# Attention and MLP on one core: loads in 512-byte runs, and a new order of the first steps

## The chip, the cores and the metric

The kernel runs on one core of a Trainium2 chip. The metric is the time of one execution in microseconds (us), measured on the device; for each kernel the median of several runs is given. Five engines of the core work side by side, each through its own queue and in the order in which its instructions stand there: TensorE (PE, with its weight loads as PEld) does the matrix products, VectorE (DVE) and ScalarE (ACT) the work on elements, GpSimd (POOL) element work that doesn't touch PSUM, and SyncE (SP) issues transfers. Matrix products land in PSUM, everything else lies in SBUF.

## The reference

Kernelized attention with random features, then a gated MLP on its output:

```python
q_s, k_s = (q * scale, k * scale)
def phi(x):
    proj = np.einsum('bhsd,md->bhsm', x, omega)
    sq = np.sum(x * x, axis=-1, keepdims=True) / 2.0
    h = proj - sq
    h = h - np.max(h, axis=-1, keepdims=True)
    return np.exp(h) / np.sqrt(m)
q_p, k_p = (phi(q_s), phi(k_s))
kv = np.einsum('bhsm,bhsd->bhmd', k_p, v)
z = np.sum(k_p, axis=2)
num = np.einsum('bhsm,bhmd->bhsd', q_p, kv)
den = np.einsum('bhsm,bhm->bhs', q_p, z)[..., None] + 1e-06
...
g = x @ w_gate
silu = g * (1.0 / (1.0 + np.exp(-g)))
out = silu * (x @ w_val) @ w_out
```

q, k and v have 8 batches, 8 heads, 576 positions and 64 dimensions in float32; omega has 128 features. The MLP sees 4608 rows of 512 and is 1536 wide. Its weights arrive as 64-bit floats, and the kernel makes float32 of them from their halves.

## The kernel before

**Groups and steps.** A group is two heads (a pair) by 256 positions, or, for the last 64 positions of each head, one group of all eight heads ("rest"). Each batch has 9 groups of keys and 9 of queries. A step handles two groups. The first AHEAD = 6 steps take two key groups each; from step 6 on a step pairs one query group with one key group; the last ones have two query groups. There are 72 steps.

**One step of the attention.** load (L340) brings the step's q and k rows into nat, load_v (L348) its v rows into one of eight tiles that have a column of ones behind each head's 64 columns (L311 to L314). load_group (L325) puts positions 2p and 2p + 1 of the group on partition p, one transfer of 128 KB for a full group, four for a rest group. st_transpose (L363) transposes nat on PE (pt), squares it on POOL (sq, L377) and copies the transposed rows on ACT (x, L378). st_project (L382) multiplies by omega on PE (pp, L393; its 16 records are one step's). st_max (L399) sums the squares on DVE (L404), takes the rows' maxima from PSUM (L411), and makes the bias of the exponentials of both with two small instructions (L413, L414). st_exp (L417) makes eight exponentials on ACT (ph, L425). k_accumulate (L510) adds the products of ph and v on PE to kvacc, two steps later; the ones give z as column 64. When a batch's four heads are complete, kv_finalize (L438) copies kvacc to SBUF (kvr); for batches 4 to 7 it also has PE transpose z (zp, L447) and sends it through memory to all partitions (zt, L464). q_transpose, q_mult, q_den, q_norm and q_out make the attention's output of ph of the queries.

**Buffers that tie the steps together.** nat has three buffers, so the load for step n + 3 waits for step n's transposes and squares. The projection of an even early step uses the two buffers of ps_p, that of an odd one two of ps_m's four; each is free again when the step's exponentials are done.

**Weights.** convert_all (L247) is a generator. Each of the 36 pieces loads 512 KB raw (load_raw, L218), takes the absolute value on ACT (L260), five DVE instructions (L262 to L270), a POOL addition (L272), and for the first nine pieces a split in a high and a low part (L242, L243); a copy goes to memory (L275). A tick advances it by one of seven stages. How many ticks are due when step n ends is interpolated over `clock` between `marks` (L202), pairs of a step and a number of pieces: (0, 0), (21, 6), (23, 9) and more. Step 21 (EARLY) is the first at which the MLP has its input.

**What sets the order of the work.** The program issues a step's parts in the order CLOSE before step 21 and GROUPED after it, with ticks and MLP work between them (L798 to L814). From that program a list scheduler makes each engine's final order at build time by its own estimate of when an instruction is ready; the chip runs each queue in that order. So an instruction whose data come later than estimated holds up those behind it on its engine. Ahead of the loop (L790 to L797) stand the loads of steps 0 to 2, omega's setup (L301: two transfers into both halves of a tile, a transpose, a scaled copy omT) and v of step 0, all issued by SP. The MLP (stream, L683) multiplies with high and low parts, three products for one (mm1 L641, mm2 L650).

Of the kernel before, what the change touches and what calls it, by code (L numbers as in the profile page):

```python
# [11 lines left out]
F32 = mybir.dt.float32  # L12
# [11 lines left out]
def kernel(  # L24
# [16 lines left out]
    P = 128  # L41
# [83 lines left out]

    def pairs_of(gr):
        return [(2 * c, 2 * c + 1) for c in range(CH)] if gr is None else [gr[:1]] * CH

# [89 lines left out]
    def load_raw(n):  # L218
        if n < 3 * NF:
            f, i = divmod(n, 3) if n >= 3 * FA else (n % FA, n // FA)  # L220
            w = (wg32, wv32, wo32)[i]
            raw = att.tile([P, 2 * DM], I32, name=f"st{f}_{i}", tag="stw")
            raws[n] = f, i, raw
            if i < 2:
                nc.sync.dma_start(
                    raw.rearrange("p (c f) -> p c f", f=2 * P),
                    w[:, f * 2 * P : (f + 1) * 2 * P].rearrange("(c p) f -> p c f", p=P),
                )
            else:
                nc.sync.dma_start(raw, w[f * P : (f + 1) * P, :])  # L230

    weights = {}
    converted = set()
# [66 lines left out]

    def setup_omega():  # L301
        om2 = accp.tile([P, 2, D], F32, name="om2", tag="acc")
        for j in range(2):
            nc.sync.dma_start(om2[:, j, :], omega)
        pt = ps_moe("pt_om", [P, M])
        nc.tensor.transpose(pt, om2.rearrange("p a d -> p (a d)"), ident)
        nc.scalar.activation(omT, pt, AF.Copy, scale=SCALE)

    vtile = [att.tile([P, CH, 2, VW], F32, name=f"v{i}", bufs=1) for i in range(NVF)]  # L311
    vrest = [att.tile([P, 2 * CH, 2, VW], F32, name=f"vrest{i}", bufs=1) for i in range(1)]
    for t in vtile:
        nc.gpsimd.memset(t[:, :, :, D:VW], 1.0)  # L314
    for t in vrest:
        nc.gpsimd.memset(t, 0.0)
        for c in range(CH):
# [4 lines left out]
    nats = {}  # L322
    busy = []

    def load_group(t, src, b, gr, v_):  # L325
        if gr is not None:
            pr, r = gr
            nc.sync.dma_start(
                t[:, :, :, 0:D],
                src[b, 2 * pr : 2 * pr + 2, r : r + G, :].rearrange("h (p c) d -> p c h d", c=CH),  # L330
            )
            return
        for c in range(CH):
            for j, pr in enumerate(pairs_of(gr)[c]):
                nc.sync.dma_start(
                    t[j * RES : (j + 1) * RES, 2 * c + j if v_ else c, :, 0:D],
                    src[b, 2 * pr : 2 * pr + 2, S - RES : S, :].rearrange("h p d -> p h d"),
                )
# [6 lines left out]
            for i, b, _, gr in slots(n, kind):  # L345
                load_group(nats[n][:, i], src, b, gr, False)

    def load_v(n):  # L348
        for i, b, g, gr in slots(n, "k"):
            rest = gr is None  # L350
            ts = (vtile, vrest)[rest]
            t = ts[nv[rest] % len(ts)]
            nv[rest] += 1
            assert t not in busy, "v's tile is still needed"
            busy.append(t)
            vrows[b, g] = t
            load_group(t, v, b, gr, True)

    box = {}
    sts = {}  # L360
# [38 lines left out]
    def st_max(n):  # L399
        if n >= NS:  # L400
            return
        st, sq, pp = sts[n]

        nc.vector.tensor_reduce(  # L404
            st[:, 0].rearrange("p i c h -> p (i c h)"),
            sq.rearrange("p i c h d -> p (i c h) d"),
            axis=AX.X,
            op=ALU.add,
        )
        for hh in range(2):  # L410
            nc.vector.tensor_reduce(st[:, 1, :, :, hh], pp[hh], axis=AX.X, op=ALU.max, negate=True)  # L411
        s0, s1, s2, s3 = (st[:, j].rearrange("p i c h -> p (i c h)") for j in range(4))
        nc.vector.scalar_tensor_tensor(s2, s0, SQC, s1, op0=ALU.mult, op1=ALU.add)  # L413
        nc.vector.scalar_tensor_tensor(s3, s0, -SQC, s2, op0=ALU.mult, op1=ALU.add)  # L414
        return True
# [21 lines left out]

    def kv_finalize(b, a2):  # L438
        acc = kvacc.pop((b, a2))
        raw = att.tile([P, 4, VW], F32, name=f"kvr{b}_{a2}", tag="kvr", bufs=4)  # L440
        nc.scalar.copy(raw, acc)
        for j in range(2):
            kvst[b, 2 * a2 + j] = raw[:, 2 * j : 2 * j + 2, :]
        if b >= BPOOL:

            zp = ps_att(f"zp{b}_{a2}", [4, P])
            nc.tensor.transpose(zp, raw[:, :, D], ident)  # L447
# [23 lines left out]
    def q_den(n):  # L471

        n -= JLAG
        for _, b, g, gr in slots(n, "q"):
# [10 lines left out]
            else:  # L485
                pr = gr[0]
                zt = zbc[b, pr // 2][:, 2 * (pr % 2) : 2 * (pr % 2) + 2, :]
                nc.gpsimd.tensor_tensor(
                    jk, ph, zt.rearrange("p (o h) m -> p o h m", o=1).broadcast_to([P, CH, 2, M]), op=ALU.mult
                )  # L490
            dn = att.tile([P, 3, CH, 2], F32, name=f"dj{b}_{g}", tag="dj", bufs=6)
            nc.vector.tensor_reduce(dn[:, 0], jk, axis=AX.X, op=ALU.add)
# [17 lines left out]
    def k_accumulate(n, half):  # L510
# [3 lines left out]
        for b, g, gr, c in ks[half * len(ks) // 2 : (half + 1) * len(ks) // 2]:  # L514
# [4 lines left out]
            for j, pr in enumerate(pairs_of(gr)[c]):  # L519
                a2 = pr // 2  # L520
                first = (b, a2) not in kvacc
                if first:
                    kvacc[b, a2] = ps_k.tile([P, 4, VW], F32, name=f"kvacc{b}_{a2}", tag="kv")
                acc = kvacc[b, a2]
                done.setdefault((b, a2), []).append(pr)
                last = LAST[pr] == (g, c)
                for hh in range(2):
                    nc.tensor.matmul(  # L528
                        acc[:, 2 * (pr % 2) + hh, :],
                        ph[:, c, hh * M : (hh + 1) * M],  # L530
                        vt[:, 2 * c + j if gr is None else c, hh, :],
                        start=first and hh == 0,
                        stop=last,
                        skip_group_check=True,
                    )
                if len(done[b, a2]) == NACC:
                    kv_finalize(b, a2)
# [4 lines left out]

    def q_transpose(n):
        m = n
        todo = [(b, g) for _, b, g, gr in slots(n - TLAG, "q") if b < BPOOL]
        todo += [(b, g) for _, b, g, gr in slots(n - NLAG, "q") if b >= BPOOL]
        for b, g in todo:
            ph = box.pop(("q", b, g))
            pt = (ps_moe if m < EARLY else ps_att)(f"ptq{b}_{g}", [P, 2, G])
            for hh in range(2):  # L550
                for c in range(CH):
                    nc.tensor.transpose(pt[:, hh, c * P : (c + 1) * P], ph[:, c, hh * M : (hh + 1) * M], ident)  # L552
# [294 lines left out]
```

## Time and profile before

| what | us |
|---|---|
| median of 3 runs | 1251.25 |
| lowest and highest run | 1250.28 and 1261.83 |
| the profiled execution, its time | 1254.07 |
| the profiled execution, first to last instruction (span) | 1252.3 |
| PE busy in it | 1217.5 |
| DVE, ACT, POOL busy | 530.8, 599.4, 506.3 |
| mean granted clock of PE | 0.988 |

A line of the timeline gives the start in us, the length in us, the engine, the line of the kernel, the operation, the tile written and the tiles read with their shape, and how many instructions were merged; in brackets stands how long the engine was idle before and for what it waited. SPq is SP's queue issuing a transfer. In the table of stretches each engine has its busy time with the number of instructions, then come the granted clock of PE (1.00 is full), the mean busy share of the 16 DMA engines, and GB/s. In the groups by line "| busy us, mean ns | idle us" stand behind the count; in the list of waits the total, the times and the longest.

### The profile page before, as it was taken

Reading aid. Unit: us, or ns where it says so; the run is one execution under the profiler, and the core shown is the slowest. Engines: PE = TensorE matmul, PEld = TensorE weight load, DVE = VectorE, ACT = ScalarE, POOL = GpSimd, SP = SyncE. Lnnn points to the kernel's source line nnn. Section 1 sums busy time; section 2 is a strip of 40 time slices with the busy share of each in tenths; the row PEclk is TensorE's granted clock in tenths of the full one; section 3 lists DMA queues with packets and bytes.
Section 4 is the critical chain, followed back from the end, with each engine's and each line's share of the span. In section 5 each row is a group of like instructions: output and inputs, shape, how many; then the busy total and the mean of one; then the engine's idle time right before and its main releaser. Section 6 shows DMA issues by size and latency. Waiting matters only on the chain.

```text
span 1252.3 us, 19047 instructions
## 1 busy us (share of the span) xinstructions
PE 1217.5 (97%) x7137; PEld 1013.1 (81%) x7137; DVE 530.8 (42%) x1080; ACT 599.4 (48%) x1344; POOL 506.3 (40%) x448
## 2 busy tenths in 40 slices
PE   6999999999999999999999998999999999999998
PEld 5988877888778888778788876888787778888887
DVE  4887696556752344334434342233433311111112
ACT  3787755554354554556555443564644323221211
POOL 3333443645362213445544432554654314242421
PEclk7999999999999999999999998999999999999999
DMA  6555555343442222222222321221211111010112
GB/s 162 146 122 157 149 135 176 105 141 115 127 126 64 53 71 64 66 66 63 73 52 60 82 52 31 69 59 52 58 43 34 36 24 51 26 51 26 51 31 54
DMA packets 157692, 97.80 MB, mean 78 GB/s; under 512 B 119680, under 2 KB 132000, under 8 KB 157600
## 3 DMA queue, kind: packets, MB, share of 16 engines
q1 hardware_dynamic: 157600, 96.59, 29.0%
q8 instruction: 56, 0.92, 0.3%
q14 instruction: 36, 0.29, 0.1%
HBM read 77.66 MB, written 18.89 MB: 77 GB/s over the span
## 4 chain that ended last, share of the span: by engine, by line
PE 68%; DVE 2%; POOL 1%; ACT 1%; issue 0%; DMA 0%; SPq 0%; POOLq 0%; DVEq 0%
PE o L650 19%; PE g L641 19%; PE v L641 19%; PE pp L393 3%; PE kvacc L528 2%; PE ptq L552 2%; PE xt L607 2%; PE pt L370 1%; PE po L569 1%; POOL hl L725 1%; DVE st L266 0%; DMA nat<-in_k_dram 0%; DVE sl L721 0%; ACT ph L425 0%; DVE st L411 0%
## 5 line engine op out<-in xcount | busy, mean ns | idle before, releaser
L725 POOL TENSOR_TENSOR hl<-sl,hh 128x512 fp32r<-128x512 f32 (+1 forms) x120 | 142.3, 1190 | 208.0 <-ACT hh L724 207.9
L641 PE MATMUL g<-xh,whi 128*128 128x512 f32 (+1 forms) x480 | 181.6, 379 | 1.7 <-DVE sl L721 1.7
L641 PE MATMUL v<-xh,whi 128*128 128x512 f32 (+1 forms) x480 | 180.1, 375 | 2.7 <-DVE acc L674 2.7
L641 PE MATMUL g<-xh,wlo 128*128 128x512 f32 (+1 forms) x480 | 178.1, 372 | 0.0
L641 PE MATMUL g<-xl,whi 128*128 128x512 f32 (+1 forms) x480 | 178.1, 371 | 0.0
L243 POOL TENSOR_TENSOR wlo<-wraw,whi 128x512 fp32r<-128x512 f32 x108 | 139.0, 1299 | 95.6 <-ACT whi L242 94.1
L641 PE MATMUL v<-xh,wlo 128*128 128x512 f32 (+1 forms) x480 | 177.4, 370 | 0.0
L641 PE MATMUL v<-xl,whi 128*128 128x512 f32 (+1 forms) x480 | 177.3, 369 | 0.0
L650 PE MATMUL o<-whi,hh 128*128 128x512 f32 x432 | 173.4, 401 | 2.8 <-ACT hh L724 2.8
L425 ACT ACTIVATE ph<-pp,st 128x128 f32<-128x128 f32 x576 | 157.9, 384 | 32.8 <-DVE st L414 32.5
L650 PE MATMUL o<-whi,hl 128*128 128x512 f32 x432 | 170.6, 395 | 2.4 <-POOL hl L725 2.4
L650 PE MATMUL o<-wlo,hh 128*128 128x512 f32 x432 | 169.8, 393 | 0.0
L724 ACT CAST hh<-sl 128x512 fp32r<-128x512 f32 (+1 forms) x120 | 69.5, 581 | 207.5 <-DVE sl L721 207.1
L721 DVE TENSOR_TENSOR sl<-v,sl 128x512 f32<-128x512 f32 (+1 forms) x120 | 75.7, 633 | 181.3 <-PE v L641 179.3
L674 DVE TENSOR_TENSOR acc<-o,acc 128x512 f32<-128x512 f32 x108 | 74.1, 689 | 185.1 <-PE o L650 185.0
L377 POOL TENSOR_TENSOR sq<-nat 128x512 f32<-128x512 f32 x72 | 77.8, 1081 | 179.2 <-DMA nat<-in_k_dram 132.0
L411 DVE TENSOR_REDUCE st<-pp 128x4 f32<-128x512 f32 x144 | 93.7, 683 | 51.2 <-PE pp L393 51.0
L242 ACT CAST whi<-wraw 128x512 fp32r<-128x512 f32 x108 | 66.4, 623 | 100.0 <-PE v L641 61.2
L641 PEld LDWEIGHTS v<-xh,whi 128*128 128x128 f32 x480 | 90.6, 189 | 20.1 <-DVE acc L674 3.1
L641 PEld LDWEIGHTS g<-xh,whi 128*128 128x128 f32 x480 | 90.9, 190 | 19.7 <-issue 2.7
L641 PEld LDWEIGHTS g<-xh,wlo 128*128 128x128 f32 x480 | 91.0, 190 | 16.0 <-issue 0.4
L641 PEld LDWEIGHTS v<-xh,wlo 128*128 128x128 f32 x480 | 90.5, 189 | 15.2
(67 smaller groups left out, 1886.0 us busy)
## 6 DMA issues: line engine op xcount, KB each, us to landing
wraw<-wscr SPq DMA_DIRECT2D x108, 256.0 KB, 2.7
wscr<-wc SPq DMA_DIRECT2D x36, 256.0 KB, 2.3
out_dram<-acc SPq DMA_DIRECT2D x72, 128.0 KB, 2.3
nat<-in_k_dram SPq DMA_DIRECT2D x64, 128.0 KB, 3.0
v<-in_v_dram SPq DMA_DIRECT2D x64, 128.0 KB, 3.0
nat<-in_q_dram SPq DMA_DIRECT2D x64, 128.0 KB, 2.7
st<-in_moe_w_gate_dram SPq DMA_DIRECT2D x12, 512.0 KB, 5.2
st<-in_moe_w_val_dram SPq DMA_DIRECT2D x12, 512.0 KB, 4.2
```

Source lines behind the costliest of these rows:

```text
L242: nc.scalar.copy(hi, raw)
L243: nc.gpsimd.tensor_tensor(lo, raw, hi.bitcast(F32), op=ALU.subtract)
L377: nc.gpsimd.tensor_tensor(sq, nat, nat, op=ALU.mult)
L393: nc.tensor.matmul(pp[hh][:, i, c, :], x[r, i, c * P : (c + 1) * P], omT[r], start=True, stop=True)
L411: nc.vector.tensor_reduce(st[:, 1, :, :, hh], pp[hh], axis=AX.X, op=ALU.max, negate=True)
L425: nc.scalar.activation(ph[:, c, hh * M : (hh + 1) * M], pp[hh][:, i, c, :], AF.Exp, bias=st[:, 3, i, c, hh : hh + 1], scale=1.0,)
L641: nc.tensor.matmul(ps, a_[:, ws], b_[:, c, :], start=n == 0, stop=n == 3 * NC - 1)
L650: nc.tensor.matmul(ps, a_[:, ts_], b_, start=first and n == 0, stop=last and n == 2)
L674: nc.vector.tensor_tensor(a_, po, a_, op=ALU.add)
L721: nc.vector.tensor_tensor(h, pv, h, op=ALU.mult)
L724: nc.scalar.copy(hh, h)
L725: nc.gpsimd.tensor_tensor(hl, h, hh.bitcast(F32), op=ALU.subtract)
```

## The change

Six edits. (1) load_group takes both positions of a partition as one run: nat and v are laid out by head and then position, so a run is 128 elements or 512 bytes and not 64 or 256. Head and position change places in everything computed from them; `place` says which index is which. (2) For this v's tile holds per head a one, the 64 columns of the even position, the 64 of the odd one, and a one; a product takes the 65 columns that end or begin with a one. kvacc gets 66 columns, z is the sum of columns 0 and 65, and POOL adds them after the copy in kv_finalize. (3) st_max issues the maxima ahead of the squares' sums, and in the first six steps the scheduler may not turn that round. (4) omega's load is one transfer issued by ACT, and the first v's loads are issued by ACT. (5) The marks get a pair (4, 0): no ticks are due ahead of step 4. (6) The first raw weight load is pinned behind the SP instruction that stands ahead of it in the program.

```diff
+    def place(gr, c, hh):
+        return (c, hh) if gr is None else (hh, c)
...
-    marks = [(0, 0.0), (EARLY, 2 * FA), (EARLY + 2, 3 * FA)]
+    marks = [(0, 0.0), (AHEAD - 2, 0.0), (EARLY, 2 * FA), (EARLY + 2, 3 * FA)]
...
+            if n == 0:
+                tc.keep_in_program_order(got)
...
-        for j in range(2):
-            nc.sync.dma_start(om2[:, j, :], omega)
+        nc.scalar.dma_start(om2, omega.rearrange("m (o d) -> m o d", o=1).broadcast_to([M, 2, D]))
...
-    vtile = [att.tile([P, CH, 2, VW], F32, name=f"v{i}", bufs=1) for i in range(NVF)]
+    vtile = [att.tile([P, 2, 1 + CH * D + 1], F32, name=f"v{i}", bufs=1) for i in range(NVF)]
...
-            nc.sync.dma_start(
-                t[:, :, :, 0:D],
-                src[b, 2 * pr : 2 * pr + 2, r : r + G, :].rearrange("h (p c) d -> p c h d", c=CH),
+            eng.dma_start(
+                t[:, :, 1 : 1 + CH * D] if v_ else t.rearrange("p h c d -> p h (c d)"),
+                src[b, 2 * pr : 2 * pr + 2, r : r + G, :].rearrange("h (p c) d -> p h (c d)", c=CH),
             )
...
-        nc.vector.tensor_reduce(
+        for hh in range(2):
+            top = nc.vector.tensor_reduce(st[:, 1, :, :, hh], pp[hh], axis=AX.X, op=ALU.max, negate=True)
+        sums = nc.vector.tensor_reduce(
...
-        for hh in range(2):
-            nc.vector.tensor_reduce(st[:, 1, :, :, hh], pp[hh], axis=AX.X, op=ALU.max, negate=True)
+        if n < AHEAD:
+            tc.add_manual_dep(
+                sums.ins,
+                top.ins.name,
...
-        raw = att.tile([P, 4, VW], F32, name=f"kvr{b}_{a2}", tag="kvr", bufs=4)
-        nc.scalar.copy(raw, acc)
+        both = att.tile([P, 4, 1 + VW], F32, name=f"kvr{b}_{a2}", tag="kvr", bufs=4)
+        nc.scalar.copy(both, acc)
+        raw = both[:, :, 1:]
+        nc.gpsimd.tensor_tensor(raw[:, :, D], raw[:, :, D], both[:, :, 0], op=ALU.add)
...
+                    e, o = place(gr, c, hh)
+                    z = 0 if gr is not None and c == 0 else 1
                     nc.tensor.matmul(
-                        acc[:, 2 * (pr % 2) + hh, :],
-                        ph[:, c, hh * M : (hh + 1) * M],
-                        vt[:, 2 * c + j if gr is None else c, hh, :],
+                        acc[:, 2 * (pr % 2) + hh, z : z + VW],
+                        ph[:, e, o * M : (o + 1) * M],
+                        vt[:, 2 * c + j, hh, :] if gr is None else vt[:, hh, c * VW : (c + 1) * VW],
...
-    for n in range(2):
-        load(n)
-        if n == 0:
-            setup_omega()
+    load(0)
+    setup_omega()
+    load(1)
     for n in range(LAV):
-        load_v(n)
+        load_v(n, nc.scalar)
```

The other lines of the diff put `place` into q_transpose, turn the order of the broadcast in q_den, and give the tiles of v two memsets where one was.

More of the change, by code (lines that the diff above doesn't have):

```diff
@@ L409, in st_max @@
         )
-        for hh in range(2):
-            nc.vector.tensor_reduce(st[:, 1, :, :, hh], pp[hh], axis=AX.X, op=ALU.max, negate=True)
+        if n < AHEAD:
+            tc.add_manual_dep(
+                sums.ins,
+                top.ins.name,
+                mybir.DependencyInfo(mybir.DependencyClass.NoSync, mybir.DependencyReason.DATA),
+                reason="the first maxima are waited for, these sums are not",
+            )
         s0, s1, s2, s3 = (st[:, j].rearrange("p i c h -> p (i c h)") for j in range(4))
@@ L551, in q_transpose @@
                 for c in range(CH):
-                    nc.tensor.transpose(pt[:, hh, c * P : (c + 1) * P], ph[:, c, hh * M : (hh + 1) * M], ident)
+                    e, o = place(gr, c, hh)
+                    nc.tensor.transpose(pt[:, hh, c * P : (c + 1) * P], ph[:, e, o * M : (o + 1) * M], ident)
             qts[b, g] = att.tile([P, 2, G], F32, name=f"qt{b}_{g}", tag="qt")
```

23 lines of the change are left out of this document (12 added, 11 removed).

## The prediction

> **What bounds the kernel now.** First the page's head and the busy time by stretch, to see where TensorE (PE) isn't the bound.
>
> ```profile
> span 1252.3 us, 19047 instructions
> ...
> PE 1217.5 (97%) x7137; PEld 1013.1 (81%) x7137; DVE 530.8 (42%) x1080; ACT 599.4 (48%) x1344; POOL 506.3 (40%) x448
> ...
> 16.00:18.00 2.00, 0.00 (x0) 0.00 (x0) 1.21 (x4) 0.00 (x0) 0.00 (x0) 0.52 1.11 341
> ...
> 30.00:32.00 2.00, 2.00 (x15) 1.78 (x13) 1.14 (x2) 0.03 (x1) 0.00 (x0) 0.50 0.01 5
> ...
> 34.00:36.00 2.00, 2.00 (x25) 1.88 (x25) 1.44 (x3) 1.97 (x8) 1.29 (x1) 1.00 0.27 59
> 46.00:111.00 65.00, 62.02 (x580) 56.06 (x579) 54.17 (x138) 52.91 (x163) 24.96 (x22) 0.97 0.57 144
> 111.00:1252.00 1141.00, 1121.19 (x6309) 926.32 (x6308) 451.80 (x896) 524.37 (x1116) 463.79 (x393) 1.00 0.27 72
> ```
>
> After 111 us PE is busy 1121 of 1141 us, from 46 to 111 us 62 of 65. The matrix work there is unchanged, so it moves as a block: what the start gives or takes is what the end shows. At 16 to 18 us only DVE works, and the granted clock of PE (the column after POOL) falls to 0.52; it is still 0.50 at 30 to 32 us and 1.00 from 34 on. So second the timeline of PE at the start, by steps of the attention (pp x16 is one step's projection; the first row is steps 0 and 1, then 2, 3, 4, 6 and 8).
>
> ```profile
> 7.99 3.79 PE L393 MATMUL pp<-omT,x 64*128 64x128 f32 x32
> ...
> 13.30 0.96 PE L370 MATMUL pt<-ident,nat 128*128 128x128 f32 x4 [0.48 <-DMA nat<-in_k_dram]
> 19.29 2.48 PE L528 MATMUL kvacc<-v,ph 128*128 128x65 f32 x10 [5.03 <-ACT ph L425]
> 21.70 2.67 PE L393 MATMUL pp<-omT,x 64*128 64x128 f32 x16
> ...
> 28.75 2.08 PE L393 MATMUL pp<-omT,x 64*128 64x128 f32 x16
> ...
> 33.93 1.16 PE L393 MATMUL pp<-omT,x 64*128 64x128 f32 x16
> ...
> 41.48 1.16 PE L393 MATMUL pp<-omT,x 64*128 64x128 f32 x16
> ...
> 48.95 1.16 PE L393 MATMUL pp<-omT,x 64*128 64x128 f32 x16
> ```
>
> PE stands 5.03 us for the first exponentials (ph), then projects at half pace (2.67 and 2.08 us against 1.16) until step 4. Steps 0 and 1 (3.79 for two) ran at half pace too, though the profile shows 1.00 there. Third, why ph is late: ScalarE (ACT) and VectorE (DVE) in order of time.
>
> ```profile
> 12.91 0.58 ACT L378 COPY x<-pt 128x512 f32<-128x512 f32 x1 [4.23 <-PE pt L370]
> 18.32 0.66 ACT L260 ACTIVATE wc<-st 128x512 f32<-128x512 f32 x1 [4.83 <-DMA st<-in_moe_w_gate_dram]
> 18.88 4.22 ACT L425 ACTIVATE ph<-pp,st 128x128 f32<-128x128 f32 x16
> ...
> 12.59 0.69 DVE L404 TENSOR_REDUCE st<-sq 128x8 f32<-128x512 f32 x1 [3.37 <-POOL sq L377]
> 13.19 1.28 DVE L411 TENSOR_REDUCE st<-pp 128x4 f32<-128x512 f32 x2
> 15.01 0.69 DVE L404 TENSOR_REDUCE st<-sq 128x8 f32<-128x512 f32 x1 [0.54 <-POOL sq L377]
> ...
> 16.29 0.15 DVE L414 SCALAR_TENSOR_TENSOR st<-st 128x8 f32<-128x8 f32 x1
> ```
>
> Two queues are in the wrong order. On DVE the maxima of step 0 (13.19) stand behind the squares' sums of step 2 (12.59), which wait for step 2's keys; the projection they read ended about 1.9 us after 7.99. On ACT the exponentials have their bias at 16.44 and stand behind the first weight conversion (L260), which waits 4.83 us for a weight load. Fourth, what loads first.
>
> ```profile
> 0.74 1.28 ACT L307 ACT_TABLE_LOAD   x1 [0.74 <-PEq L831]
> ...
> 0.88 0.33 POOL L314 MEMSET v<- 128x4 f32 x8
> ...
> 4.88 1.04 POOL L377 TENSOR_TENSOR sq<-nat 128x512 f32<-128x512 f32 x1 [2.40 <-DMA nat<-in_k_dram]
> ...
> 0.75 1.45 SPq L328 DMA_DIRECT2D nat<-in_k_dram  x2
> 2.24 1.11 SPq L304 DMA_DIRECT2D om<-in_omega_dram  x2
> 3.39 1.30 SPq L328 DMA_DIRECT2D nat<-in_k_dram  x2
> 4.74 1.34 SPq L328 DMA_DIRECT2D v<-in_v_dram  x2
> ...
> 26.69 0.38 SPq L225 DMA_DIRECT2D st<-in_moe_w_gate_dram  x1
> ...
> L464 SPq DMA_DIRECT2D zt<-zd x8: 325/332/348, 404.0 to 901.3; - x8
> ```
>
> An issue of 256 B runs keeps SP 0.65 us, one of 1 KB runs 0.38, one of 512 B runs (zt) 0.33.
>
> **The change, part by part.**
>
> *Omega and first v on ScalarE.* SP loses 1.11 + 1.34 us of issues: step 1's keys go out 1.15 us earlier, step 2's and all behind them 2.45. ACT takes three issues of about 0.65 ahead of its table load; 0.74 + 2.0 + 1.28 = 4.0 us, before omega's transpose gives it work, so they are hidden. If that cover went, each would cost its 0.65. Omega no longer holds PE until 5.18: the transposes of step 0 start with its keys, 4.8. They and step 1's (0.25 each at half pace) and the copy of x end near 6.9, so pp starts at 6.9 instead of 7.99.
>
> The pages have a rule against this edit: the Trainium skill, "DMA: Bandwidth & Descriptors", section "Issuing engines are not separate DMA queues", says that transfers from several engines interleave on the same 16 DMA engines and only issue time is saved. By it omega and v would delay step 0's keys; at the 341 GB/s of the row at 16 us their 320 KB last 1 us, and the time below would be 1 us longer. Here SP alone issues, so no row shows it.
>
> *Maxima before sums.* pp of step 0 ends at 6.9 + 1.9 = 8.8; maxima 1.28, sums 0.69, two small ones 0.31: bias at 11.1. The copy of x for step 2, which ACT has ahead of the exponentials (12.91 before), then waits for PE (pp of step 1 to 10.7, transposes about 1): 11.3 to 12.0. I take the exponentials' start between the two, 11.6 instead of 18.88: **-7.3 us**, from -6.9 to -7.8. The first projection that needs the buffers they free (step 2) followed 2.8 us behind and still does: 14.4 instead of 21.70. What is late next is that release, then the clock.
>
> *The clock.* Step 2 to 6 took 41.48 - 21.70 = 19.8 us, mostly at half clock; step 4 to 8 took 48.95 - 33.93 = 15.0 at full clock. The drop at 16 us came in the gap of PE from 14.26 to 19.29. Now PE has transposes of steps 2 and 3 until about 12.5 and the first ph at 12, so the gap nearly closes: **-4.8 us**, or 0 if the clock falls anyway.
>
> *Weights from step 4.* Two costs. The first load comes when the exponentials of steps 4 and 5 are queued behind L260; who waits for those is the projection two steps on and PE behind it. The wait is between 0 and the 4.83 us of today; in the row at 18.32 it hit with its full length because the order of ACT counts on a load's estimated landing; this load has the shorter queue ahead, so I take 1.0: **+1.0**. Then conversion: up to step 6 the due ticks are 14 before (2 a step), now 8 (2.47 a step from step 4, rounded up); step 21 wants 42 either way. So 6 ticks of 7 a piece move into steps 7 to 20.
>
> ```profile
> L270 DVE SCALAR_TENSOR_TENSOR wc<-st,wc 128x512 f32<-128x512 uint32 x21 | 17.7, 844 | 0.2
> L266 DVE SCALAR_TENSOR_TENSOR st<-st,wc 128x512 int32<-128x512 int32 x21 | 15.4, 732 | 0.2
> L262 DVE TENSOR_SCALAR wc<-wc 128x512 f32<-128x512 f32 x22 | 12.8, 580 | 15.1 <-ACT wc L260 15.0
> L268 DVE TENSOR_SCALAR wc<-st 128x512 int32<-128x512 int32 x21 | 11.0, 523 | 0.2
> L264 DVE TENSOR_SCALAR wc<-wc 128x512 int32<-128x512 int32 x21 | 10.0, 478 | 0.1
> ```
>
> A piece is 844 + 732 + 580 + 523 + 478 = 3157 ns of DVE, six sevenths are 2.7 us. DVE is busy 54.2 of 65 us there and PE 62, so between 0 and 2.7; I take **+1.2**, nearer to hidden.
>
> *Runs of 512 B.* SP saves about 0.3 us on each of 192 big loads (0.65 to 0.33 or 0.38). On the path are only the first: step 0's second load goes out 0.3 earlier, at most -0.5 in all. The rest is hidden behind PE:
>
> ```profile
> PE pt L370 <- DMA nat<-in_k_dram: 1.0, 2, 0.5
> ...
> PE o L650 <- ACT hh L724: 2.8, 1, 2.8
> ...
>   PEld zp L447: 1.0, 4
> ...
> 745.37 3.11 POOL L484 TENSOR_TENSOR jk<-ph,zt 64x256 f32<-64x256 f32 x4 [5.64 <-ACT ph L425]
> ```
>
> PE waits 1.0 us in all for keys, so I take 0; if that cover were gone the gain would grow by the same 1.0. The new place of heads and chunks in ph changes no shape. Eight more memsets (0.33 us for eight) lie in POOL's idle 2.40 ahead of 4.88.
>
> *The second column of ones.* Sixteen small POOL additions behind the copy of kvacc. For batches under 4 the sum is needed steps later. For the other eight finalizations PE transposes z right behind the copy (PEld waits 1.0 us in 4 of them), so the addition now stands between. Its price is not in the trace: from 0 (PE has MLP work to put first) to 8 times a POOL in the middle of the 3.11 us group, 26 us. Near the small end, **+0.5**.
>
> **The sum.** -7.3 - 4.8 + 1.0 + 1.2 + 0.5 = -9.4 us. The profiled execution lasted 1254.07 (span 1252.3 and 1.8 around it), which becomes 1244.7. It lies 2.8 above the median of the runs, 1251.25, so for the median I predict 1241.9, 0.75% faster.
>
> **The rivals.**
>
> *Half clock stays.* If PE's pauses before the exponentials still add up, the 4.8 are lost: 1251.25 - 7.3 + 2.7 = 1246.7. For it: PE was busy from 19.29 on and the clock was still 0.50 at 32 us. Against: the pause falls from 5.03 to under 1 us. The Trainium skill, "TensorE: Matmul & The Clock Gate", section "What's actually happening", says that an idle window of about 3.4 us halves the clock; the trace agrees (5.03 us of pause, 0.52 in the row of 16 us).
>
> *All costs hidden, and later waits shorter too.* L260 finds its weights landed, the ticks hide, and the one long late wait of PE (2.8 us for hh) goes because loads land sooner: 1251.25 - 7.8 - 4.8 - 0.5 - 2.8 = 1235.4. For it: DVE has 11 us free from 46 to 111. Against: that wait hangs on an order of issue.
>
> *No gain.* Loads not pinned (the second weight load) are moved ahead of keys, or the new order only moves the waiting to step 2's data: 1251. Against: the waits removed are of known length.
>
> *Slower: z behind POOL.* The instruction order lets PE reach z's transpose while POOL still has a queue ahead of the addition. At 3.11 + 0.2 us for each of eight finalizations: 1241.9 - 0.5 + 26.5 = 1267.9. It decides from 2.8 us each on ((12.5 + 9.9) / 8 for +1%). For it: nothing else on POOL is ordered for this. Against: a wait of one such place would have to repeat at all eight.
>
> **How the numbers follow.** Chances: the forecast 0.50 (its own range 1237 to 1246), half clock 0.20, all hidden 0.17, no gain 0.08, slower 0.05. A measurement of this kernel tells about 1%, 12.5 us, from no change. Faster by over 1% means under 1238.7: all hidden (0.17) and the lower part of the forecast (0.18), 0.35. Slower by over 1%: 0.05. The rest 0.60. The range holds the forecast, half clock and most of all hidden: 1231 to 1249; left out are no gain, slower, and tails.
>
> **What would show it.** Right: exponentials starting at 11 to 12.5 us with no weight conversion ahead; no pause of PE over 2 us before 20 us; granted clock 1.00 from 14 us on; pp of step 6 near 29 to 31 us; SP issues of q, k and v at 0.33 to 0.4. Wrong: a wait of ACT for the gate weights of several us near 20 to 26 us; pp still over 2 us at step 3; DVE over 9 tenths in steps 7 to 20 with the lead shrinking; PEld waiting over 5 us in all at zp.

## The result, and the profile after

| kernel | median, us | lowest and highest | runs |
|---|---|---|---|
| before | 1251.1 | 1248.4 and 1261.8 | 18 |
| after | 1269.8 | 1261.9 and 1281.5 | 18 |

The ratio is 1.0136, with a 95% interval of 1.0117 to 1.0155: the change makes the kernel slower, by 18.7 us in the medians and by 17 in the ratio, where 9.3 us faster was predicted. Where an execution of a series was disturbed, its ratio leaves it out, and so do the medians of e8, e10 and e11 below. The profiled execution of the kernel after lasted 1262.65 us, near the fast end. Its span is 8.6 us longer than that of before, and these 8.6 are what the trace can place; no trace shows where a median run loses the rest.

First the head of the page after, then the busy time by stretch (columns as in the prediction; the one after POOL is PE's granted clock).

```profile
span 1260.9 us, 19088 instructions
...
PE 1227.1 (97%) x7137; PEld 1016.5 (81%) x7137; DVE 542.3 (43%) x1080; ACT 600.1 (48%) x1344; POOL 514.3 (41%) x472
```

```profile
12.00:14.00 2.00, 0.00 (x0) 0.00 (x0) 1.58 (x5) 0.00 (x0) 0.00 (x0) 0.70 0.88 242
16.00:18.00 2.00, 1.27 (x8) 0.83 (x6) 0.00 (x0) 1.69 (x6) 0.68 (x1) 0.50 0.36 99
30.00:32.00 2.00, 2.00 (x11) 1.92 (x10) 0.00 (x0) 0.00 (x0) 0.00 (x0) 0.50 0.44 127
38.00:40.00 2.00, 2.00 (x18) 1.82 (x15) 0.87 (x2) 0.24 (x1) 0.00 (x0) 0.50 0.80 210
46.00:111.00 65.00, 60.34 (x562) 54.01 (x561) 60.53 (x138) 52.68 (x161) 33.39 (x31) 0.97 0.57 164
111.00:1252.00 1141.00, 1127.40 (x6358) 929.85 (x6355) 463.65 (x909) 530.26 (x1137) 469.22 (x405) 1.00 0.25 71
```

Behind 111 us PE is busy nearly all the time, as before. The loss lies ahead: 7.8 of the 8.6 us are there when step 20 is projected (113.8 against 106.0 us, in the table further down). The clock falls by 14 us already and is still 0.50 at 38 to 40 us; before it was at 1.00 from 34 on. Then PE's timeline, the rows that answer to those of the prediction.

```profile
6.84 3.25 PE L403 MATMUL pp<-omT,x 64*128 64x128 f32 x32
...
14.88 1.34 PE L380 MATMUL pt<-ident,nat 128*128 128x128 f32 x4 [4.20 <-DMA nat<-in_k_dram]
16.95 0.80 PE L403 MATMUL pp<-omT,x 64*128 64x128 f32 x4 [0.73 <-ACT x L388]
...
33.05 0.80 PE L403 MATMUL pp<-omT,x 64*128 64x128 f32 x4 [0.73 <-ACT x L388]
...
45.36 0.49 PE L403 MATMUL pp<-omT,x 64*128 64x128 f32 x4 [0.73 <-ACT x L388]
```

The first projection starts at 6.84, as forecast (6.9). Then PE stands 4.20 us again, now for the keys of step 3. Step 2 is projected at 16.95 instead of 21.70, but step 6 at 45.36 instead of 41.48. The reason is in ACT's order, here its timeline.

```profile
10.78 0.59 ACT L388 COPY x<-pt 128x512 f32<-128x512 f32 x1 [3.25 <-PE pt L380]
16.31 0.58 ACT L388 COPY x<-pt 128x512 f32<-128x512 f32 x1 [4.95 <-PE pt L380]
16.79 4.24 ACT L442 ACTIVATE ph<-pp,st 128x128 f32<-128x128 f32 x16
28.25 0.58 ACT L388 COPY x<-pt 128x512 f32<-128x512 f32 x1 [7.22 <-PE pt L380]
32.41 0.58 ACT L388 COPY x<-pt 128x512 f32<-128x512 f32 x1 [3.58 <-PE pt L380]
32.89 4.24 ACT L442 ACTIVATE ph<-pp,st 128x128 f32<-128x128 f32 x16
...
37.57 0.66 ACT L269 ACTIVATE wc<-st 128x512 f32<-128x512 f32 x1 [0.17 <-DMA st<-in_moe_w_gate_dram]
```

The bias of step 0 is ready at 12.65 (the small DVE instruction of L431, 0.15 us from 12.50); no weight conversion stands ahead of the exponentials. But the copies of x for steps 2 and 3 do, and the second waits 4.95 us for step 3's transposes. The same pattern repeats: x of steps 4 and 5 (28.25, 32.41), then the exponentials of 2 and 3. In the kernel before, the exponentials stood ahead of x of step 3 and steps followed one another; now **they go in pairs**, each pair's exponentials behind the next pair's copies. Why step 3's keys are late is in SP's queue: first the kernel before, then the kernel after.

```profile
9.43 0.65 SPq L328 DMA_DIRECT2D v<-in_v_dram  x1
10.20 1.29 SPq L328 DMA_DIRECT2D nat<-in_k_dram  x2
```

```profile
6.31 0.98 SPq L338 DMA_DIRECT2D v<-in_v_dram  x2
7.41 2.56 SPq L345 DMA_DIRECT2D vrest<-in_v_dram  x4
10.01 2.13 SPq L338 DMA_DIRECT2D v<-in_v_dram  x4
12.25 2.96 SPq L338 DMA_DIRECT2D nat<-in_k_dram  x6
```

Step 3's keys go out at 10.20 before and at 12.25 after, though SP was relieved of 2.45 us: ten issues of values, of steps 1 to 4, now stand ahead of them. Before it was one, besides those of step 0.

**How much is order, how much is the clock.** A run's mean granted clock c tells how long PE was at half: 2 (1 - c) of its span. The fastest run after (1261.94 us, clock 0.986, span 1260.1) was 35 us at half, the slowest that the ratio counts (1276.95, 0.970, 1275.2) 77 us. A straight line through the 17 runs that it counts gives 0.40 us of time for one of half clock (correlation 0.98). The median run after has 56 us at half, one of the kernel before 27.5 to 30, by series. By that line 10 to 11 us of the 18.7 are more half clock, and some 7 or 8 are there at any clock. This split is an estimate: in the other series of six and more runs the same line has slopes from 0.08 (e3) to 0.47 (e10, e18).

### The profile page after: what moved, and what is told of

It is laid out like the page before. It is cut to its first block, busy times and chain, and to the rows that moved or that the text cites. A ratio compares the mean times of both kernels' runs of the same rounds, so it can differ in the third digit from the quotient of the medians.

```text
span 1260.9 us, 19088 instructions
## 1 busy us (share of the span) xinstructions
PE 1227.1 (97%) x7137; PEld 1016.5 (81%) x7137; DVE 542.3 (43%) x1080; ACT 600.1 (48%) x1344; POOL 514.3 (41%) x472
## 4 chain that ended last, share of the span: by engine, by line
PE 68%; DVE 2%; POOL 1%; ACT 1%; issue 0%; POOLq 0%; ACTq 0%; DVEq 0%
PE o L673 19%; PE v L664 19%; PE g L664 19%; PE pp L403 3%; PE kvacc L550 2%; PE ptq L575 2%; PE xt L630 2%; PE pt L380 1%; PE po L592 1%; POOL hl L748 0%; ACT ph L442 0%; DVE st L415 0%; DVE st L275 0%; DVE st L431 0%; DVE st L416 0%
## 5 line engine op out<-in xcount | busy, mean ns | idle before, releaser
L403 PE MATMUL pp<-omT,x 64*128 64x128 f32 x1152 | 107.4, 302 | 3.3 <-ACT x L388 3.3
L403 PEld LDWEIGHTS pp<-omT,x 64*128 64x128 f32 x1152 | 88.6, 200 | 24.3 <-issue 12.8
```

Source lines behind the costliest of these rows:

```text
L403: nc.tensor.matmul(pp[hh][:, i, c, :], x[r, i, c * P : (c + 1) * P], omT[r], start=True, stop=True)
```

## The experiments

All are the kernel before or after with edits; medians and ratios stand against runs of the kernel before on the same chip (1250.8 to 1251.3 us).

| run | median, us | ratio to before, 95% interval |
|---|---|---|
| e1 sums first again | 1260.9 | 1.0047 to 1.0101 |
| e2 loads pinned | 1261.4 | 1.0038 to 1.0118 |
| e3 weights as before | 1262.7 | 1.0073 to 1.0130 |
| e4 only 512 B | 1259.3 | 1.0040 to 1.0100 |
| e8 the rest without 512 B | 1264.0 | 1.0059 to 1.0125 |
| e5 after, order written out to step 8 | 1251.9 | 0.9983 to 1.0015 |
| e6 before, the same order | 1251.5 | 0.9981 to 1.0024 |
| e7 only 512 B, the same order | 1264.6 | 1.0085 to 1.0128 |
| e9 e5 with weights from step 2 | 1254.2 | 0.9998 to 1.0040 |
| e10 e5 without DVE's conversion work | 1252.5 | 0.9987 to 1.0032 |
| e11 e5 with sums first | 1261.7 | 1.0048 to 1.0118 |
| e12 e5 without 512 B | 1250.0 | 0.9954 to 1.0006 |
| e13 e5, PE filled in steps 7 to 20 | 1277.8 | 1.0140 to 1.0255 |
| e14 e5, PE filled in steps 0 to 6 | 1251.4 | 0.9991 to 1.0034 |
| e15 both fillings | 1281.8 | 1.0202 to 1.0287 |
| e16 after, order written out to step 22 | 1249.4 | 0.9941 to 0.9993 |
| e17 e16 with 15 useless products | 1245.0 | 0.9918 to 0.9965 |
| e18 before, order to step 22 | 1250.4 | 0.9966 to 1.0021 |

**One part at a time (e1 to e4, e8).** e1 puts st_max back as before. e2 pins the loads of q, k and v for the first steps behind one another. e3 takes out the pair (4, 0) and the pin of the first weight load. e4 is the kernel before with the 512 B layout and one transfer of omega alone, e8 the kernel before with all but the layout.

```diff
+            if pins[0]:                       # e2, in load_group, n + LA < 8
+                tc.keep_in_program_order(got)
...
-    marks = [(0, 0.0), (AHEAD - 2, 0.0), (EARLY, 2 * FA), (EARLY + 2, 3 * FA)]
+    marks = [(0, 0.0), (EARLY, 2 * FA), (EARLY + 2, 3 * FA)]     # e3
```

e1: 

> The changed kernel with the squares' sums ahead of the maxima again; all else as changed. Theory A (order): asking for maxima first makes the list scheduler place step 3's copy ahead of the first exponentials on ACT and step 3's projection ahead of step 2's on PE, so that steps run in pairs in lockstep; then this run is near the kernel before, 1246 to 1254 us, with exponentials of steps 2 and 3 apart from each other. Theory B (loads): ten v issues stand ahead of step 3's keys on SP, PE pauses 4 us, the clock halves; those stay here, so 1260 us or more. Theory C (weights): conversions moved into steps 7 to 20 overload DVE; that stays too, 1260 us or more.

e2: 

> The changed kernel with every load of q, k and v up to step 7 pinned in program order, so that step 3's keys go out ahead of the v of steps 1 to 3. Theory B (loads): no pause of PE before the first exponentials, which start at 12.7 us instead of 16.8; clock full from 13 us on; 1240 to 1250 us. Theory A (order): the first exponentials come at 12.7 us too, but pp of step 3 still stands ahead of step 2's and steps 2 and 3 still go in a pair; 4 us better at most, 1257 to 1266 us. Theory C: 1258 to 1266 us.

e3: 

> The changed kernel with the marks of before and no pin: weights are converted from step 0 on. Theory C (deferred conversions crowd DVE in steps 7 to 20, where the changed kernel falls another 8 us behind): that lag goes, 1254 to 1262 us. Theories A and B: the lag at step 8 stays or grows because the first conversion again stands in ACT ahead of the first exponentials; 1262 to 1275 us.

e4: 

> The kernel before with the runs of 512 B (and the two columns of ones) alone: omega and first v by SP, sums first, conversions from step 0. All theories that blame the order of the first steps: the order of maxima is that of before, so near before, 1246 to 1255 us. If the 512 B layout itself costs (the POOL additions ahead of z, the unaligned rows of v, the scheduler's other estimate of loads): 1258 us or more, with waits at zp or kvacc that before does not have.

e8: 

> The kernel before with the order of the vector work, omega and first values issued by the scalar engine, the pinned weight load and the conversions from step 4, but with runs of 256 B as before. If the layout's share is additive, it is near 1262 us (1269.8 less 8). If the pairs of steps come from the order of the vector work alone, they are there too (exponentials 2 near 33 us). If the layout is what makes the scheduler change the order, the time is near that of before or under it, 1242 to 1251.

e1, e2 and e3 each give 7 to 9 us back and none gives all; together that is 24 us, more than was lost, so the parts aren't independent. (The layout alone costs 8, the rest alone 13, both 18.7.) In e1 the steps no longer go in pairs (exponentials of step 2 from 26.26 us, of step 3 from 32.66), which ties the pairs to the maxima's new place. But PE still stands 4.33 us for step 3's keys, the first exponentials start at 18.97, and the range for theory A (1246 to 1254) is missed. In e3 the pairs stay, and a conversion that waits 6.02 us for its weights again stands ahead of a copy of x. e2 is the clearest: with keys ahead of values the exponentials start at 12.86 us and PE's long pause is gone, yet the steps stay in pairs and the time is 1261.4. So the late keys aren't the whole. In e4 the layout, which was to cost nothing, changes SP's order in another way: both first weight loads go out at 8.75 us, ahead of step 3's keys. ACT's timeline of e4, then PE's:

```profile
13.12 0.66 ACT L266 ACTIVATE wc<-st 128x512 f32<-128x512 f32 x1 [7.06 <-DMA st<-in_moe_w_gate_dram]
13.68 0.57 ACT L385 COPY x<-pt 128x512 f32<-128x512 f32 x1
```

```profile
14.30 2.08 PE L400 MATMUL pp<-omT,x 64*128 64x128 f32 x16 [6.01 <-ACT x L385]
```

A conversion that waits 7.06 us for its weights stands ahead of x of step 1, and PE stands 6.01. No profile of e8 is read. Its time, of three runs, is near what adding the shares gives (1262) and shows that the layout isn't needed for a loss.

**The order written out (e5 to e7).** The loads up to step 7 are pinned, x of step n + 1 goes behind the exponentials of step n - 1, and a step's projection behind that of the step before, up to step 8.

```diff
-        nc.scalar.copy(x, pt)
+        xc = nc.scalar.copy(x, pt)
+        if 3 <= n <= 8:
+            behind(xc, lastexp[n - 2])
...
+                    if n <= 8:
+                        if n and (i, c, hh) == (0, 0, 0):
+                            behind(mm, lastpp[n - 1])
```

e5: 

> The changed kernel with the order of its first eight steps written out: loads in program order, x of step n+1 copied only behind the exponentials of step n-1, and the projections of a step begun only behind those of the step before (both up to step 8). All parts of the change stay. If the loss is the order of the first 50 us (late keys, steps in pairs), exponentials 0 and 1 start near 12.9 and 14.9 us and those of step 2 near 21 to 24 instead of 32.9, the projections of step 6 near 32 to 36 instead of 45.4, and the time is 1240 to 1250 us. If the 512 B layout or the conversions from step 4 cost by themselves, the projections of step 6 are early but the lead is gone by step 20 and the time stays at 1255 to 1262.

e6: 

> The kernel before with the same order written out and no part of the change. It is a control: if writing the order out does nothing by itself, 1248 to 1253 us, and the first exponentials stay near 18 to 19 us because a weight conversion stands ahead of them. If the tighter order costs something by itself (steps that no longer overlap), it is slower, 1255 us or more.

e7: 

> The kernel with only the 512 B layout and the one load of omega, and the same order written out. The layout alone, in the order that was built for it, was 8 us slower than before. If that was the order alone, it comes to the time of the kernel before in this order (1248 to 1253). If the layout costs by itself (the transfers, the rows with a stride of 130 words in the products), it stays 6 to 8 us above it.

e5 takes back the whole loss, with every part of the change in place: 1251.9, with 32 us at half clock in the median run. The control e6 shows that writing the order out does nothing to the time of the kernel before. So **the loss is the order**, shown. e7 came out above both of its ranges: its order on SP was written out for q, k and v only, the two weight loads are ahead of step 3's keys as in e4, and PE stands 5.55 us for x of step 1. It is no evidence against the layout: e12, below, is. But e5 isn't faster either, though its early steps are what was forecast:

```profile
13.25 1.47 PE L570 MATMUL kvacc<-v,ph 128*128 128x65 f32 x10 [1.00 <-ACT ph L462]
14.65 2.48 PE L419 MATMUL pp<-omT,x 64*128 64x128 f32 x16
...
34.82 1.16 PE L419 MATMUL pp<-omT,x 64*128 64x128 f32 x16 [0.62 <-ACT x L402]
```

Step 2 at 14.65 (forecast 14.4), step 6 at 34.82, 6.7 us ahead of the kernel before; by step 17 the lead is gone (92.7 against 91.0 us). The next runs ask where.

**Where the lead goes (e9 to e12).** e9 begins the conversions at step 2. e10 leaves four of DVE's five instructions out of the first nine pieces. e11 puts the sums first, e12 takes the layout out.

e9: 

> The changed kernel in the written-out order (1251.9 us), with its conversions begun at step 2 instead of step 4. If the lead of 6.7 us that the written-out order has at step 6 is eaten by conversions that now crowd steps 6 to 18 on VectorE, two conversions in the idle VectorE time of steps 2 to 4 keep about 2 us of it and one spell of half clock less: 1244 to 1249 us. If the clock's spells come from elsewhere, 1250 to 1254.

e10: 

> The written-out order again, but four of the five VectorE operations are left out of the conversion of the nine first weight pieces (the range limits and the shifts and masks that rebuild the exponent), so the weights and the output are wrong; loads, stores, ScalarE's and GpSimd's work stay. About 9 x 4 x 0.45 us = 16 us of VectorE work less before step 21. If VectorE's crowding in steps 6 to 20 gives the lead back, the lead at step 6 is still there at step 20 (the projections of step 20 near 99 to 101 us, before 106.0), half clock between 50 and 130 us is nearly gone, and the time is 1236 to 1243. If the lead is lost to PE's own work and to the clock whatever VectorE does, 1248 to 1253.

e11: 

> The written-out order with the sums of squares ahead of the maxima, as the kernel before has them. By the order built, the sums of steps 0 to 4 then all stand ahead of the last work of step 0 on VectorE. If that matters, the exponentials of step 0 start near 18 to 24 us instead of 12.8 and the time is 1254 to 1262; if the sums are ready in time, no difference from 1251.9.

e12: 

> The written-out order with all parts of the change but the 512 B runs. If the layout is worth something once the order is fixed, this is slower than 1251.9 (SP issues of 0.65 us: the keys of steps 3 and 4 about 1.5 to 2.5 us later, 1252 to 1256). If the layout's shifted ones and the added GpSimd operation cost something, it is faster, 1245 to 1250.

e9 and e10 contradict the idea that spreading or dropping conversions keeps the lead, but e10 doesn't settle it: behind step 8 its order is free, and there ACT's casts of the weights wait for POOL (4.5 us in all from 36 to 90 us) with x copies behind them, and PE stands 6.5 us for x from 36 to 112 us. One wait took the place of another. e11 is 10 us slower than e5, but this isn't the price of the maxima's place alone: step 6 comes 2.2 us later than in e5 (37.00 against 34.82), step 8 5.7 (50.27 against 44.57) and step 20 11.2 (123.39 against 112.21), so about half of it grows behind the held steps. At the start DVE has the sums of steps 0 to 3 ahead of the first maxima, and the first exponentials start at 14.58 instead of 12.83:

```profile
11.31 0.69 DVE L434 TENSOR_REDUCE st<-sq 128x8 f32<-128x512 f32 x1 [1.11 <-POOL sq L401]
11.91 1.28 DVE L441 TENSOR_REDUCE st<-pp 128x4 f32<-128x512 f32 x2
```

e12 and e5 can't be told apart: whatever the 512 B layout gains or costs here is within the noise, some 4 us.

**Filling PE (e13 to e15).** Useless products of ident by ident, pinned behind PE's previous instruction, their result read by nobody.

```diff
+                tc.keep_in_program_order(
+                    nc.tensor.matmul(spare[0], ident, ident, start=spare[1], stop=spare[1], skip_group_check=True)
+                )
```

e13: 

> The written-out order (1251.9 us) with useless products of ident by ident on PE, two at each of three places in each of steps 7 to 20 (76 in all, 0.11 us each at full clock, 8.3 us), written to columns of the accumulator's bank that nobody reads. If the lead is lost because short pauses of PE bring spells of half clock, the pauses are partly filled, the half clock between 50 and 130 us falls from 20.5 us to under 7, and the time is 1243 to 1249 in spite of the added work. If pauses and the clock have nothing to do with each other, half clock stays and the time rises by about the added work less the pauses that it fills, to 1254 to 1260.

e14: 

> The written-out order with 40 useless products on PE in steps 0 to 6 alone: six before omega has landed, five while x of step 0 is copied, eight and then three at each place in the pauses before the first accumulations (4 to 8 us in all). If pauses bring the half clock, the spell of 10.2 us from 15 us is gone or shorter, the projections of step 6 come at 31 to 35 us, and the time is 1246 to 1251; later spells stay. If not, the spell stays and step 6 is 2 to 5 us later.

e15: 

> Both sets of useless products. By the clock theory the half clock before 130 us is under 10 us (written-out order: 30.7) and the time 1240 to 1247, under the kernel before, for the order's lead is kept. By the other theory, that PE's work and the chain through the other engines set the time whatever the clock, 1255 us or more.

e13 missed both of its ranges, and neither e13 nor e15 decides: a product is two records on PE, each 0.11 us behind the one before, so it costs 0.22 us and not 0.11. PE had some 17 us more to do by step 20 and the steps came late; the half clock (47 and 44 us in the median) didn't fall. e14 did what the clock theory says: in its profile the clock is 1.00 from 13 to 27 us, the median's half clock fell from 32.5 to 22.5 us, and the added work ate the gain.

**The order to step 22 (e16 to e18).** e16 is e5 with 22 for 8. e17 adds 15 products where PE waits anyway. e18 is the control.

```diff
+        fill(6)                                       # ahead of omega's transpose
+        fill(4 if n == 0 else 0)                      # in st_project
+        if half == 0:
+            fill(5 if n == 2 else 0)                  # in k_accumulate
```

e16: 

> The written-out order carried on to step 22 instead of step 8, without useless products. If the lead of step 6 is lost because the scheduler's order is free again after step 8 (the steps pair up, as in the profile of the changed kernel), it is kept to step 17 and the time is 1243 to 1248. If it is lost to pauses and the clock in any order, 1250 to 1256; if a rigid order adds pauses, more.

e17: 

> The changed kernel with the order written out to step 22 (1249.4 us), and 15 useless products on PE where it waits anyway: six before omega has landed, four while x of step 0 is copied, five in the pause ahead of the first accumulation. The heavier set of 40 in steps 0 to 6 took the median's half clock from 32.5 to 22.5 us but added 8.5 us of work by step 6. If the first spell (13 to 27 us in the profile of the written-out order) comes from that first pause, it is gone for about 2 us of work: half clock 10 us less at 0.4 us each, 1244 to 1248, under the kernel before. If the pause has nothing to do with it, 1249 to 1252.

e18: 

> The kernel before with only the order written out to step 22. If the changed kernel in that order (1249.4) owes its small gain to the order alone, this one is at 1248 to 1251 as well, and the parts of the change are worth nothing in the end; if the parts of the change (earlier first exponentials, shorter issues) are worth something when the order is held, it is slower by 1 to 4 us, 1250.5 to 1253.5.

e17 beats both kernels: 1245.0 us, ratio 0.9941 (0.9918 to 0.9965). Its median run has 24 us at half clock, e16's 32, which at 0.40 would be 3.5 of the 4.4 us between them. Their intervals overlap, so these 4.4 us aren't clear of noise. e16, between its two ranges, and e18 can't be told apart (1249.4 and 1250.4): with the order held, the change's parts are worth about 1 us, if anything.

## Why the prediction was wrong, by its steps

Two steps failed, and one premise.

**"Maxima before sums ... the exponentials' start between the two, 11.6": failed.** They start at 16.79. The sum took ACT's and SP's queues as those of the kernel before, with one copy (x of step 2) ahead of the exponentials and step 3's keys going out early. But the order is made anew from the whole program, and in the new one ten value loads came ahead of the keys and x of step 3 ahead of the exponentials. e1 ties the second to the maxima's place; what moved the value loads no run isolates. The rival "no gain" named loads that are moved ahead of keys, and gave them a price that only takes the gain away and a chance of 0.08; the order cost 18.7. With the order held (e5) they start at 12.83; the 1.2 us still missing are DVE's, which puts step 1's two maxima ahead of and between the small instructions of step 0, the first of which takes 0.63 us (bias at 12.65 to 12.8, not 11.1).

**"The clock: -4.8": failed, with the wrong sign.** It counted on PE's pause before the first accumulations nearly closing, and on a short one being harmless. In the kernel after PE pauses 4.20 us, for step 3's keys. With the order held the pause is 1.00 us (e5) or 1.69 (e16), and the clock falls all the same. The stretches of e16, then of e17, cut at the clock's steps:

```profile
10.00:13.40 3.40, 1.71 (x17) 1.35 (x15) 3.37 (x8) 1.34 (x4) 1.15 (x2) 1.00 0.50 128
13.40:16.80 3.40, 3.40 (x20) 3.28 (x21) 0.91 (x2) 3.40 (x15) 0.93 (x1) 0.50 0.77 211
23.60:27.00 3.40, 3.40 (x22) 3.18 (x21) 2.57 (x5) 0.58 (x1) 0.68 (x1) 0.50 0.11 32
...
95.30:98.71 3.41, 1.83 (x17) 1.62 (x16) 3.41 (x5) 2.30 (x9) 1.10 (x1) 1.00 0.37 117
98.71:102.12 3.41, 3.41 (x33) 3.05 (x32) 2.14 (x9) 2.12 (x6) 1.35 (x2) 1.00 0.50 135
```

```profile
27.60:31.00 3.40, 2.16 (x20) 2.02 (x19) 1.48 (x3) 1.63 (x6) 1.04 (x1) 1.00 1.09 345
31.00:34.40 3.40, 2.98 (x21) 2.76 (x21) 3.02 (x8) 3.21 (x11) 1.69 (x2) 0.51 0.44 107
```

In e16 a stretch with PE half busy (1.71 of 3.40) is followed by 13.6 us at half, though PE is busy throughout. In e17 the products carry PE over that place, the clock stays at 1.00 to 31 us, step 6 comes at 31.4, and the spell follows there instead, after a pause of 1.66 us at 30 us behind a weight load. So a pause of 1 to 2 us can cost 10 to 17 us at half, 4 to 7 us of time at 0.40. It need not: in the last two rows of e16 PE is busy 1.83 us, hardly more, and the clock stays at 1.00. Take all traces but e8's, cut into stretches of 3.41 us at the clock's steps, and of these the ones at full clock. All 49 with PE busy under 1.5 us are followed by half clock, 17 of 38 with 1.5 to 2.1 us, 15 of 195 with 2.1 to 3.0, and none of 6418 above. What decides in the middle is open. The Trainium skill, "TensorE: Matmul & The Clock Gate", section "What's actually happening", gives free-running windows of 3413 ns; the traces agree (the spells in the clock's records, 10.24, 13.65 and 17.07 us among them, are multiples of it). Its section "HAM oscillation — how this bites in real kernels" sets the limit at pauses over about 3.4 us; here 1 to 2 us in one window were sometimes enough.

**The premise that from the start on the work "moves as a block, what the start gives ... is what the end shows": failed between steps 6 and 20.** The table takes PE's records up to a step's first projection: the time without any (idle), and the busy time at half clock (ahead of the first record of the clock too, where the rows run at half pace).

| kernel | step 6 at | idle | at half | step 20 at | idle | at half |
|---|---|---|---|---|---|---|
| before | 41.5 | 11.3 | 20.9 | 106.0 | 14.5 | 24.3 |
| after | 45.4 | 10.8 | 28.7 | 113.8 | 16.1 | 32.1 |
| e5 | 34.8 | 6.4 | 17.1 | 112.2 | 14.5 | 37.6 |
| e16 | 35.4 | 6.3 | 19.0 | 104.8 | 14.3 | 22.0 |
| e18 | 40.7 | 11.6 | 18.4 | 104.3 | 14.4 | 18.4 |

What remains when the idle time and half of the last column are taken off is 79 to 82 us at step 20 in all of them. Behind step 20 the premise holds to some 6 us: from there to the end the five take 1141 to 1147 us. Up to step 6, e16 has 5.3 us less idle time than e18, as forecast. By step 20 both have 14.3 to 14.4: the lead is returned as idle time of PE. The profile says to whom, by stretches from step 6 to 12 and 12 to 20; first e16, then e18.

```profile
35.43:64.40 28.97, 25.08 (x230) 22.27 (x230) 27.88 (x62) 22.98 (x70) 15.88 (x15) 0.94 0.55 153
64.40:104.80 40.40, 36.35 (x351) 32.24 (x350) 36.88 (x87) 32.22 (x98) 19.74 (x17) 1.00 0.58 169
```

```profile
40.70:66.10 25.40, 23.98 (x244) 21.94 (x243) 20.58 (x53) 21.69 (x68) 9.54 (x9) 1.00 0.63 160
66.10:104.30 38.20, 36.87 (x351) 33.14 (x350) 30.61 (x87) 32.26 (x98) 15.82 (x14) 1.00 0.60 151
```

With the conversions put off, **DVE is busy 27.88 of 28.97 us in steps 6 to 12** (it has 18 conversion instructions there, e18 has 10), and these steps take 3.6 us longer, the next eight 2.2. From step 6 to 20 the conversions take 23.9 us of DVE (36 instructions) against 12.4 (24) in e18, and the two small instructions of st_max 11.3 against 5.2. The first is the term of the deferred conversions, "+1.2", bounded by 2.7; the second had no term. By these rows they come to about 5.8 us of time together and eat the lead; some half clock is in it too (0.94 against 1.00 in the first stretch). The bound counted ticks at their durations of before, and both were off; the last section has why the durations were. That DVE is what holds these steps is read from the rows; no run isolated it, since e10 brought another wait.

**What held.** Omega and first v on ACT: pp at 6.84. The wait of ACT for gate weights: 0.17 us after, 1.77 in e17; forecast 1.0 (the first gate weights). The additions of z on POOL cost PE almost nothing; here PE's own wait after, then that of its weight loads:

```profile
PE zp L466 <- POOL kvr L460: 0.2, 1, 0.2
...
PEld zp L466 <- POOL kvr L460: 3.2, 7, 0.6
```

Issues of 512 B runs took SP about 0.49 us (2.96 for six), not 0.33 to 0.38. The 0.33 was read off zt, whose transfers are 256 KB to 128 partitions, so 2 KB a run and not 512 B. The runs were forecast to be worth 0, and by e12 no other worth is clear of noise. Of the signs named for "wrong", pp over 2 us at step 3 and DVE over 9 tenths with a shrinking lead (60.53 of 65 us) both came. The range missed because one mechanism, the order made anew, had no price of its own among the rivals.

## What to carry to other kernels

Where a scheduler orders the queues, an edit of loads, dependencies or layout is also an edit of every queue's order: predict the order that will be built, or write it out around the change, before pricing anything. A lead at the start counts only as far as the next engine lets it through, so look at the busy share of the others in the stage that follows, and not at PE's alone. Short pauses of PE can be paid again as half clock; fill them, if at all, where PE waits anyway.

## What the runs showed of the hardware

The price of half clock, 0.40 us for each us of it, comes out of runs of one and the same kernel, the one after: it explains nearly all of their spread of 15.0 us. It is no constant; in the five series of the kernel before the slope is 0.15 to 0.34.

Small DVE instructions stretch while POOL works. DVE by line in steps 6 to 20, the same three instructions: first e16 (L451, L275, L450), then e18 (L434, L266 and L433 in that order, below by cost).

```profile
L451 DVE SCALAR_TENSOR_TENSOR st<-st 128x8 f32<-128x8 f32 x14 | 7.0, 501 | 0.0
L275 DVE SCALAR_TENSOR_TENSOR st<-st,wc 128x512 int32<-128x512 int32 x7 | 6.8, 978 | 0.0
...
L450 DVE SCALAR_TENSOR_TENSOR st<-st 128x8 f32<-128x8 f32 x15 | 4.3, 286 | 0.0
```

```profile
L266 DVE SCALAR_TENSOR_TENSOR st<-st,wc 128x512 int32<-128x512 int32 x5 | 3.4, 687 | 0.0
L433 DVE SCALAR_TENSOR_TENSOR st<-st 128x8 f32<-128x8 f32 x14 | 3.0, 217 | 0.0
L434 DVE SCALAR_TENSOR_TENSOR st<-st 128x8 f32<-128x8 f32 x14 | 2.2, 154 | 0.1
```

An instruction of 154 ns (L434) takes 501 (L451) in the mean. The timeline of e16, one row of each engine, shows how: the sums, now issued after the maxima, free the buffer of squares, POOL starts the next squares at that moment (it waited for L436), and the small instruction behind ends when POOL's does.

```profile
13.29 1.04 POOL L401 TENSOR_TENSOR sq<-nat 128x512 f32<-128x512 f32 x1 [1.37 <-DVE st L436]
...
13.44 0.91 DVE L451 SCALAR_TENSOR_TENSOR st<-st 128x8 f32<-128x8 f32 x1
```

The Trainium skill, "SBUF — State Buffer", section "SBUF: two separate sides", says that a DVE instruction with two inputs in SBUF and a POOL instruction hold a port pair in turn, the second blocked for the whole of the first; the rows agree. This is a cost of putting sums behind maxima that the prediction had not seen.
